# Inputs laid out on the host as they are read, a new order for the first batch's attention, and N of the second batch in 256 columns

## The chip, the cores and the metric

The kernel runs on one core of a Trainium2 chip. The metric is device time in microseconds from start to end of one execution; the median of three runs is given. The core has TensorE (matmul), VectorE, ScalarE, GpSimd and SyncE, which issues the DMAs. In the rows they are PE (PEld for its weight loads), DVE, ACT, POOL and SP.

## The reference

q, k, v are (4, 8, 576, 64) in float32; the weights w_in1, w_in2 (512, 2048) and w_out1, w_out2 (2048, 512) come as float64. Per batch and head a Nystrom attention with 32 landmarks is computed, then two feed-forward layers over 2304 tokens of width 512:

```
q_lm, k_lm = means over 18 tokens           # 32 landmarks each
A = softmax(q k_lm^T / 8);  B = softmax(q_lm k_lm^T / 8);  C = softmax(q_lm k^T / 8)
Z = B^T / (norm1(B) * norminf(B));  6 times: Z = 2 Z - Z B Z
x = A Z C v                                  # heads side by side: 2304 x 512
h = x w_in1;  x = (h * clip(h + 3, 0, 6) / 6) w_out1
h = x w_in2;  out = elu(h) w_out2
```

## The kernel before, in words

Except for the first half batch's product with w_out1, which is a plain float32 matmul, the layers' operands are split into a high and a low part (nh/nl, ath/atl, gh/gl, wo pairs) and three products are summed. The weights arrive as float64 and are converted on the chip: `steps` loads 512 doubles per partition into a staging tile (u, un or ub), ScalarE makes two passes, VectorE two (a shift and a combination, through a PSUM bank in the stream), GpSimd adds.

Attention and first layer are fused: M = Z C v (mt) is multiplied into w_in1 (tile w1c), giving N (`attn_n`, pair nh/nl), and a slot of the first layer multiplies N with A transposed (`attn_at`, pair ath/atl). There are 128 slots: batch b, half of the batch (288 tokens), 128 columns of the 2048. `slot_a1` makes h and the activation g (or gh/gl), `slot_a2` multiplies it with w_out1, DELAY = 3 slots later. Batch 0's attention is in `start`, whose order is the string PLAN, one letter a step: k prepares a pair of heads, a, b, c are the scores A, B, C of the first group of four heads, A, B, C those of the second, v and V the products with v, i a step of the inverse, f finish (which writes mt), n a block of N, t attn_at, x and y a conversion step on ScalarE and VectorE, w a fill matmul whose result nobody reads, digits and l load a weight unit. Batch 0's first half of slots (`first_half`) converts the rest of w_in1 and w_out1, two units per slot in most slots. In the second half the attention of batch 1 is woven in by the string PLAN1, where s is a fifth of a slot and n a block of N of batch 1. On VectorE, ScalarE, GpSimd and TensorE the instructions of this part run strictly in the written order (`InOrder`). After that a planner sets the order by due times (`wanted`): batches 2 and 3 (`newton`), and the conversion of the second layer's weights (`conv_out2`, `conv_in2`, every third slot).

The second layer works on 768 tokens at a time with a seven-product scheme (`quartet`, `second`). `load_x` fetches x in four pieces per half, forms four sums and splits seven operands; `load_in2` does the like for a slice of w_in2.

q and k in batch 0 are loaded as [96 partitions, 2 heads, 6 x 64] and turned by TensorE against an identity, after a copy that brings pairs of heads together (side); in batches 1 to 3 they are loaded in runs of 128 bytes (qkraw) and turned by VectorE in 32 x 32 blocks.

Of the kernel before, what the change touches and what calls it, by code (L numbers as in the profile page):

```python
# [31 lines left out]
def nystrom_ffn_kernel(ctx: ExitStack, tc, q, k, v, w_in1, w_out1, w_in2, w_out2, out):  # L32
# [28 lines left out]
    B, H, S, D = q.shape  # L61
    DM, DFF = w_in1.shape
    NT = B * S
    G = H // 4
# [5 lines left out]
    NDM = DM // 128  # L70
# [105 lines left out]
    def heads(x, b, g, pr):  # L176

        return x[b].rearrange("(i r) t d -> r i t d", r=G)[g, 2 * pr:2 * pr + 2]

# [18 lines left out]
    def steps(src, u, f, out=None):  # L198
# [3 lines left out]
        if isinstance(src, list):  # L202
            n = W // len(src)
            for i, x in enumerate(src):
                gated(sp.dma_start(
                    out=u[:, i * n:i * n + n].rearrange("p (k n) t -> p k (n t)", k=x.shape[1]), in_=x.bitcast(U32)
                ))
            lo, hi = u[:, :, 0], u[:, :, 1]
        elif len(src.shape) == 3:
            u = u.rearrange("p (k n) t -> p k n t", k=src.shape[1])  # L210
            sp.dma_start(out=u.rearrange("p k n t -> p k (n t)"), in_=src.bitcast(U32))
# [81 lines left out]
    ROOM = [{3: "nl1"}, {0: "nh2", 1: "nl2", 2: "nh3", 3: "nl3"}, {3: "nl3"}, {}]  # L293

    def conv_in1(c):

        def unit(o):
            if (0, c) not in w1_t:
                w1_t[0, c] = w1_tile()
            t = w1_t[0, c]  # L300
            cols = slice(c * W + o, c * W + o + 128)
            f = t[:, o // 128]
            yield from steps(w_in1[:, cols].rearrange("(k p) n -> p k n", p=128), room(ROOM[c].get(o // 128)), f)
# [29 lines left out]
    def conv_in2(m, kk):  # L333

        w = w_in2.rearrange("(h k p) (i n) -> h k p i n", h=2, p=128, i=2)[:, kk, :, :, m * 128:m * 128 + 128]
        src = [w[h, :, i:i + 1] for h, i in ((0, 0), (1, 0), (1, 1), (0, 1))]
        sp.dma_start(out=wi2d[m, kk], in_=to_f32(src, room()))
# [60 lines left out]
    def load_qk(b, g, what, prs=range(2)):  # L398
        src = k if what == "k" else q
        for pr in prs:  # L400
            t = ap_.tile([128, TB, 32], F32, name="qkraw", tag="qkraw", bufs=4)
            for hp in range(2):
                for e in range(2):
                    p0 = 32 * (2 * hp + e)
                    gated(sp.dma_start(
                        out=t[p0:p0 + 32],
                        in_=heads(src, b, g, pr)[hp, :, 32 * e:32 * e + 32].rearrange("(tb t) d -> t tb d", t=32),
                    ))
            raw_t[b, g, what, pr] = t

    def load_v(b, g, tiles=None):

        if tiles is None:
            vt = ap_.tile([128, 4, RUN * D], F32, name="vt", tag="vt", bufs=1)
            tiles = [vt[:, 0:2], vt[:, 2:4]]
        for i in range(2):
            sp.dma_start(
                out=tiles[i][0:PRUN],
                in_=heads(v, b, g, i).rearrange("h (p j) d -> p h (j d)", j=RUN),
            )  # L420
# [20 lines left out]
    def landmarks(x, lm, bd):  # L441

        vec.tensor_reduce(
            out=lm, in_=x.rearrange("p (l c) -> p l c", c=POOL), axis=AX, op=ALU.add
        )
        pool.tensor_tensor(
            out=bd, in0=lm.unsqueeze(1).to_broadcast([128, 2, 32]),
            in1=maskp.unsqueeze(2).to_broadcast([128, 2, 32]), op=ALU.mult,
        )

    def lm_tiles(b, g, what):
        lm = ap_.tile([128, 2, 32], F32, name="lm", tag="lm" + what, bufs=2 if what == "k" else 1)
        if what == "k":
            kl_t[b, g] = lm
        t = ap_.tile([128, 2, 2, 32], F32, name="bd", tag="bd", bufs=3)
        (kbd_t if what == "k" else qbd_t)[b, g] = t
        return lm, t

    def prep(b, g):

        for what, dst in (("k", kt_t), ("q", qt_t)):
            x = ap_.tile([128, 2, S], F32, name=what + "t", tag=what + "t")
# [3 lines left out]
            nb, ng = (b, g + 1) if g + 1 < G else (b + 1, 0)  # L466
            if nb < B:
                load_qk(nb, ng, what)
            lm, t = lm_tiles(b, g, what)
            for pr in range(2):  # L470
                landmarks(x[:, pr], lm[:, pr], t[:, pr])
                yield 1.3
            dst[b, g] = [x[:, pr, :] for pr in range(2)]
# [5 lines left out]

    def load_first(src, g, tiles):  # L480

        for i in range(2):
            sp.dma_start(
                out=tiles[i][0:PRUN],
                in_=heads(src, 0, g, i).rearrange("h (p j) d -> p h (j d)", j=RUN),
            )
        return tiles

    def prep_first():

        JB = RUN // 2
        pairs = [(g, what, pr) for g in range(G) for what in "kq" for pr in range(2)]
        sides = []

        def beside(i):

            g, what, pr = pairs[i]
            src = raw_t[0, g, what][pr].rearrange("p h (j d) -> p j h d", d=D)
            for x in ("gh", "gl"):
                t = gp.tile([128, JB * 2 * D], F32, name="side", tag=x)  # L500
                (vec.tensor_copy if x == "gh" else act.copy)(
                    out=t[0:PRUN].rearrange("p (j h d) -> p j h d", j=JB, h=2),
                    in_=src[0:PRUN, JB * (x == "gl"):JB * (x == "gl") + JB],
                )
                sides.append(t)

        beside(0)
        beside(1)
        for i, (g, what, pr) in enumerate(pairs):
            dst = kt_t if what == "k" else qt_t  # L510
            if pr == 0:
                if g == 0:
                    n = "h" if what == "k" else "l"
                    dst[0, g] = [
                        nat.tile([128, G, W], F32, name="kq", tag=f"n{n}{2 + j}").rearrange("p g w -> p (g w)")[:, 0:S]
                        for j in range(2)
                    ]
                else:
                    t = ap_.tile([128, 2, S], F32, name=what + "t", tag=what + "t")
                    dst[0, g] = [t[:, j] for j in range(2)]  # L520
                lm, bd = lm_tiles(0, g, what)
            x = dst[0, g][pr]
            xj = x.rearrange("p (t j) -> p j t", j=RUN)
            for a in range(2):
                b = bank()[:, 0:JB * PRUN]
                for j in range(JB):
                    atr(b[:, PRUN * j:PRUN * j + PRUN], sides[2 * i + a][0:PRUN, 2 * D * j:2 * D * (j + 1)],
                        ident[0:PRUN, 0:PRUN])
                act.copy(out=xj[:, JB * a:JB * a + JB], in_=b.rearrange("p (j t) -> p j t", j=JB))
            if i + 2 < len(pairs):  # L530
                beside(i + 2)
            landmarks(x, lm[:, pr], bd[:, pr])
            yield
# [16 lines left out]
    def score_c(b, g, sc):  # L550
# [16 lines left out]
        for hf in range(2):  # L567
# [3 lines left out]
            )  # L571
        return EC

    def soft(b, g):
# [3 lines left out]
        for hf in range(2):  # L578
# [4 lines left out]
            yield 0.4  # L583
        ea = ap_.tile([128, TB, 32], F32, name="ea", tag="ea", bufs=2)
# [177 lines left out]
    PLAN = "kkkkkk3bykbykcyc1bcll02ByBBwwyxlaccwwywiyyxyaaivwwywCixyvyiylaCixviCiyyCvwyiiAyaAvAiiVAyvVvyyiVyiVyViVaiwyAiyyyyyxyfAAVwywwxwfAyxfywyyyyxnwxt"  # L762

    def start():
# [10 lines left out]

        def fill(eng):
# [9 lines left out]
            "k": prep_first, "f": lambda: finish(0, kept["Q"], cvs, sc), "n": lambda: attn_n(0, 0, 128),  # L786
            "i": lambda: keep("Q", inverse(EB, sb)),
# [9 lines left out]
        for c in PLAN.replace(" ", ""):  # L797
# [5 lines left out]
            elif c == "t":  # L803
                run(attn_at(0, 0, vec))
# [4 lines left out]
            else:  # L809
                if c not in gens:  # L810
                    gens[c] = make[c]()
                next(gens[c], None)
        return units, gens["n"]
# [246 lines left out]
    def loads(b):  # L1060
        load_v(b, 0)
        for what in "kq":
            for pr in range(2):
                yield
                load_qk(b, 0, what, [pr])
# [47 lines left out]
    PLAN1 = "ssssssuulslullslsssspppspsssppspppssssosssbbcsbsocscscsaPasvaoavsssPvvosPavPasssPossPssPPssssssssBPoCCBssCBososssisCsssisAississiAoAssissisVosiVAVVioiAsssAVisisisiioisssfftftssssnotsnTnssonnssnonsnsssnnsnnsTnnosssnnsssTssssssss"  # L1113

    def second_half(slots):
# [7 lines left out]
        def parts():  # L1123
            for c in range(NW):
                yield from attn_n(1, c, 128)
# [155 lines left out]
```

## Time and profile before

| | us |
|---|---|
| median of 3 runs | 862.93 (862.11 to 863.07) |
| the profiled execution | 861.07 |
| its span, first to last instruction | 859.2 |
| TensorE, VectorE, ScalarE, GpSimd busy | 817.8, 532.1, 465.2, 346.5 |
| mean granted TensorE clock | 0.974 |

The profiled execution's own time is 1.87 us over its span, and 1.86 us under the median. A granted clock of 1.00 is 2.4 GHz, 0.50 is 1.2 GHz; values between them are mixtures over the stretch. DMA share is the busy share of the 16 DMA engines as the profile counts it, and it can read slightly over 1.

### The profile page before, as it was taken

To read this page: it belongs to the slowest core of one execution; us is meant where nothing else is said; L and a number is where in the kernel's file an instruction comes from. 1 tells how busy PE (TensorE), PEld (TensorE's weight loads), DVE (VectorE), ACT (ScalarE), POOL (GpSimd) and SP (SyncE) were. 2 spreads that over 40 slices of the span, in tenths; PEclk is the share of its full clock that TensorE was granted. 3 is DMA by queue.
4 is the path that set the end of the run, shared out by engine and by line. 5 is a ranking of instruction groups with operands and counts; after the bars stand their busy time and mean duration, and the time that the engine had idled before them with its cause. 6 is when DMAs were issued, how large, how long until landed. Compare 5 with 4: busy or idle time off the path is not lost.

```text
span 859.2 us, 16284 instructions
## 1 busy us (share of the span) xinstructions
PE 817.8 (95%) x5896; PEld 708.2 (82%) x5896; DVE 532.1 (62%) x1080; ACT 465.2 (54%) x1048; POOL 346.5 (40%) x352
## 2 busy tenths in 40 slices
PE   7788899889999999999998899999999999999998
PEld 5556687679887788979998789999889889999996
DVE  6789687536664465445776887664665555645544
ACT  7578455444554555557565666564454444434433
POOL 1357566425553365547576885631082000000000
PEclk9969999969999999999999899999999999999999
DMA  9868996358455633366387557768665365664541
GB/s 258 263 221 290 249 179 91 104 169 211 127 156 172 225 114 103 99 194 199 128 285 263 177 184 252 272 241 300 228 212 202 135 208 209 202 229 168 172 147 73
DMA packets 167024, 165.69 MB, mean 193 GB/s; under 512 B 64801, under 2 KB 129825, under 8 KB 166945
## 3 DMA queue, kind: packets, MB, share of 16 engines
q1 hardware_dynamic: 166944, 164.66, 61.0%
q8 instruction: 46, 0.75, 0.4%
q14 instruction: 34, 0.27, 0.1%
HBM read 119.54 MB, written 45.09 MB: 192 GB/s over the span
## 4 chain that ended last, share of the span: by engine, by line
PE 68%; DVE 10%; DMA 9%; ACT 4%; issue 3%; POOL 3%; SPq 2%; DVEq 0%; POOLq 0%; ACTq 0%
PE x L104 35%; PE h L104 26%; PE bk L104 8%; DMA u<-in_moe_w_out 3%; SPq L104 2%; DMA u<-in_moe_w_in 2%; DVE y L104 1%; DVE u L104 1%; DVE h L104 1%; POOL x L104 1%; DMA out<-ob 1%; DVE gf L104 1%; DVE w1c L104 1%; DVE nl L104 1%; DMA x<-x1d 1%
## 5 line engine op out<-in xcount | busy, mean ns | idle before, releaser
L104 PE MATMUL h<-x,wi 128*128 128x384 f32 x1008 | 207.8, 341 | 7.1 <-DVE y L104 3.1
L104 PE MATMUL x<-gh,wo 128*128 128x288 f32 x896 | 205.8, 303 | 0.0
L104 PEld LDWEIGHTS h<-x,wi 128*128 128x128 f32 x1008 | 182.6, 190 | 22.7 <-DVE y L104 4.4
L104 PEld LDWEIGHTS x<-gh,wo 128*128 128x128 f32 x896 | 152.3, 191 | 15.2 <-issue 13.4
L104 PE MATMUL x<-gl,wo 128*128 128x288 f32 x448 | 134.3, 301 | 0.6 <-POOL gl L104 0.3
L104 ACT CAST gh<-gf 128x288 fp32r<-128x288 f32 (+1 forms) x172 | 79.0, 460 | 81.1 <-DVE gf L104 80.7
L104 PE MATMUL x<-w,gh 128*128 128x512 f32 x360 | 116.3, 393 | 0.0
L104 ACT ACTIVATE gf<-y 128x384 f32<-128x384 f32 x96 | 50.4, 525 | 99.2 <-DVE y L104 99.2
L104 POOL TENSOR_TENSOR gl<-gf,gh 128x288 fp32r<-128x288 f32 x84 | 68.9, 823 | 77.7 <-ACT gh L104 73.3
L104 DVE SCALAR_TENSOR_TENSOR gf<-gf,y 128x384 f32<-128x384 f32 x96 | 63.6, 663 | 57.7 <-ACT gf L104 57.6
L104 PE MATMUL h<-atl,nh 128*128 128x288 f32 x256 | 83.1, 324 | 12.5 <-DVE g L104 8.8
L104 PEld LDWEIGHTS x<-gl,wo 128*128 128x128 f32 x448 | 85.4, 191 | 6.0 <-issue 4.0
L104 PE MATMUL x<-w,ghl 128*128 128x512 f32 x324 | 89.2, 392 | 0.0
L104 ACT ACTIVATE gf<-h,half_b 128x288 f32<-128x288 f32 x128 | 64.0, 500 | 40.2 <-PE h L104 37.6
L104 PE MATMUL h<-ath,nh 128*128 128x288 f32 x256 | 78.0, 305 | 0.0
L104 DVE SCALAR_TENSOR_TENSOR gf<-gf,h 128x288 f32<-128x288 f32 x112 | 49.9, 446 | 45.2 <-ACT gf L104 44.5
L104 PE MATMUL h<-ath,nl 128*128 128x288 f32 x256 | 77.6, 303 | 0.0
L104 PEld LDWEIGHTS x<-w,gh 128*128 128x128 f32 x360 | 67.5, 189 | 9.2
L104 DVE TENSOR_TENSOR gl<-gf,gh 128x384 fp32r<-128x384 f32 (+1 forms) x88 | 59.2, 673 | 25.5 <-ACT gh L104 21.4
L104 PE MATMUL x<-w,gl 128*128 128x512 f32 x180 | 70.9, 394 | 0.0
L104 PEld LDWEIGHTS h<-atl,nh 128*128 128x128 f32 x256 | 49.9, 195 | 23.6 <-DVE g L104 13.0
L104 PEld LDWEIGHTS x<-w,ghl 128*128 128x128 f32 x324 | 60.2, 188 | 8.4
(158 smaller groups left out, 1349.3 us busy)
## 6 DMA issues: line engine op xcount, KB each, us to landing
wi<-wi2p SPq DMA_DIRECT2D x64, 448.0 KB, 4.9
w<-wo2p SPq DMA_DIRECT2D x32, 512.0 KB, 6.2
wi2p<-wi SPq DMA_DIRECT2D x32, 448.0 KB, 2.8
w1c<-w1d SPq DMA_DIRECT2D x48, 256.0 KB, 4.1
ub<-in_moe_w_out SPq DMA_DIRECT2D x16, 512.0 KB, 7.2
u<-in_moe_w_out SPq DMA_DIRECT2D x16, 512.0 KB, 4.5
wo2p<-w SPq DMA_DIRECT2D x16, 512.0 KB, 3.1
u<-in_moe_w_in SPq DMA_DIRECT2D x64, 128.0 KB, 2.8
```

The costliest lines, as they stand in the source:

```text
L104: inst = getattr(self.eng, name)(*a, **kw)
```

## The change

The host now lays q and k out as [batch, group, 128, 2, 576] (head dimension on partitions, tokens in the row), v as [batch, group, 96, 4, 384], w_in1 in blocks of 128 columns with each partition's four runs together, and w_in2 in the order in which `conv_in2` reads it. So `load_qk` is one DMA, `prep_first` with its matmuls and copies and VectorE's transposes in `prep` are gone, and one DMA replaces four in `conv_in2`. PLAN is new, k prepares both pairs of heads, and one y pair stands where there were many. N of batch 1 is made in blocks of 256 columns, with eight n in PLAN1 in place of sixteen. Not in the title: two staging places differ in ROOM, the loads of q and k for batches 2 and 3 are issued in `score_c` and `soft`, `load_x(0)` subtracts on VectorE where it used GpSimd, and `load_in2(1)` is due four slots later.

```diff
-        if isinstance(src, list):
-            n = W // len(src)
-            for i, x in enumerate(src):
-                gated(sp.dma_start(
-                    out=u[:, i * n:i * n + n].rearrange("p (k n) t -> p k (n t)", k=x.shape[1]), in_=x.bitcast(U32)
-                ))
...
+            gated(sp.dma_start(
+                out=u.rearrange("p n t -> p (n t)"), in_=src.rearrange("p k n -> p (k n)").bitcast(U32)
+            ))
...
-    ROOM = [{3: "nl1"}, {0: "nh2", 1: "nl2", 2: "nh3", 3: "nl3"}, {3: "nl3"}, {}]
+    ROOM = [{2: "nl1", 3: "nh1"}, {0: "nh2", 1: "nl2", 2: "nh3", 3: "nl3"}, {3: "nl3"}, {}]
...
-    def load_qk(b, g, what, prs=range(2)):
-        src = k if what == "k" else q
-        for pr in prs:
-            t = ap_.tile([128, TB, 32], F32, name="qkraw", tag="qkraw", bufs=4)
-            for hp in range(2):
-                for e in range(2):
...
+    def load_qk(b, g, what):
+        t = ap_.tile([128, 2, S], F32, name=what + "t", tag=what + "t", bufs=2)
+        gated(sp.dma_start(out=t, in_=(k if what == "k" else q)[b, g]))
+        raw_t[b, g, what] = t
...
             for pr in range(2):
-                gated(vec.transpose(out=x[:, pr], in_=raw_t.pop((b, g, what, pr)).rearrange("p a c -> p (a c)")))
-                yield 1.3
...
+                gated(vec.tensor_reduce(
+                    out=lm[:, pr], in_=x[:, pr].rearrange("p (l c) -> p l c", c=POOL), axis=AX, op=ALU.add
+                ))
...
-    def prep_first():
...
+        if 0 < b < B - 1:
+            load_qk(b + 1, g, "k")
         return EC
...
-    PLAN = "kkkkkk3bykbykcyc1bcll02ByBBwwyxlaccwwywiyyxyaaivwwywCixyvyiylaCixviCiyyCvwyiiAyaAvAiiVAyvVvyyiVyiVyViVaiwyAiyyyyyxyfAAVwywwxwfAyxfywyyyyxnwxt"
+    PLAN = """
+        k0k1k23bbllccllkb cc BBB CCCC aaAA ixxi vavvVivv
+        iVai iVAwwi iVAawwwi iVawwwi ixxywwwi A iywwwwii
+        ffAwwwwwtxfxwwwwntwwwwwxt
+    """
...
-    PLAN1 = "ssssssuulslullslsssspppspsssppspppssssosssbbcsbsocscscsaPasvaoavsssPvvosPavPasssPossPssPPssssssssBPoCCBssCBososssisCsssisAississiAoAssissisVosiVAVVioiAsssAVisisisiioisssfftftssssnotsnTnssonnssnonsnsssnnsnnsTnnosssnnsssTssssssss"
+    PLAN1 = "ssssssuulslullslsssspppspsssppspppssssosssbbcsbsocscscsaPasvaoavsssPvvosPavPasssPossPssPPssssssssBPoCCBssCBososssisCsssisAississiAoAssissisVosiVAVVioiAsssAVisisisiioisssfftftssssotsnTssonssnosnsssnsnsTnosssnsssTssssssss"
...
-                yield from attn_n(1, c, 128)
+                yield from attn_n(1, c, 256)
...
-                x0 = load_x(0, pool)
+                x0 = load_x(0, vec)
...
-    wanted(NA - 6)
+    wanted(NA - 2)
     load_in2(1)
...
+        if name in ("q", "k"):
+            b, h, s, d = a.shape
+            a = a.reshape(b, 2, 2, h // 4, s, d).transpose(0, 3, 2, 5, 1, 4).reshape(b, h // 4, 2 * d, 2, s)
+        elif name == "v":
+            b, h, s, d = a.shape
+            a = a.reshape(b, 4, h // 4, s // 6, 6 * d).transpose(0, 2, 3, 1, 4)
+        elif name == "moe_w_in":
+            a = a.reshape(a.shape[0] // 128, 128, a.shape[1] // 128, 128).transpose(2, 1, 0, 3)
+        elif name == "moe2_w_in":
+            a = a.reshape(2, 2, 128, 2, a.shape[1] // 256, 128).transpose(4, 1, 2, 0, 3, 5)
+            a = _np.stack([a[:, :, :, i, j] for i, j in ((0, 0), (1, 0), (1, 1), (0, 1))], axis=3)
```

## Rows read from the trace of the kernel before

**Rows 1.** The page, part 1: busy us (share of span) x instructions.
```profile
PE 817.8 (95%) x5896; PEld 708.2 (82%) x5896; DVE 532.1 (62%) x1080; ACT 465.2 (54%) x1048; POOL 346.5 (40%) x352
```
**Rows 2.** Stretches: length, busy (x instructions) by engine, clock, DMA share, GB/s.
```profile
700.00:800.00 100.00, 100.00 (x500) 90.53 (x499) 54.06 (x101) 44.53 (x89) 0.00 (x0) 1.00 0.56 196
```
**Rows 3.** VectorE in order of time: start, duration, instruction.
```profile
37.64 0.28 DVE L104 COPY mt<-bk 128x128 f32<-128x128 f32 x1
...
64.97 0.45 DVE L104 SCALAR_TENSOR_TENSOR g<-gf,h 128x288 f32<-128x288 f32 x1
...
68.88 0.45 DVE L104 SCALAR_TENSOR_TENSOR g<-gf,h 128x288 f32<-128x288 f32 x1
...
101.93 0.46 DVE L104 SCALAR_TENSOR_TENSOR g<-gf,h 128x288 f32<-128x288 f32 x1 [0.43 <-ACT gf L104]
```
**Rows 4.** Waits of TensorE, 105 to 300 us: total, times, longest.
```profile
PE bk L104 <- DVE nl L104: 5.7, 8, 0.7
```
**Rows 5.** Stretches around the N of batch 1.
```profile
160.00:170.00 10.00, 7.79 (x139) 5.35 (x139) 4.81 (x18) 5.61 (x21) 4.19 (x5) 1.00 0.47 132
170.00:180.00 10.00, 8.18 (x98) 5.67 (x98) 3.74 (x14) 3.71 (x15) 2.40 (x3) 0.65 0.76 228
180.00:190.00 10.00, 9.27 (x77) 7.64 (x76) 2.48 (x9) 4.56 (x15) 2.52 (x4) 0.66 0.23 78
```
**Rows 6.** The stretch ahead of the second layer.
```profile
385.00:445.00 60.00, 57.82 (x418) 54.79 (x417) 38.70 (x64) 38.97 (x88) 41.54 (x37) 0.97 0.57 181
```
**Rows 7.** TensorE's groups, 0 to 20 us: busy, mean ns, idle before.
```profile
L104 PE MATMUL bk<-ident,side 96*128 96x96 f32 x48 | 9.5, 373 | 5.1 <-DVE side L104 4.9
```
**Rows 8.** The first 18 us in order of time, ScalarE and VectorE.
```profile
3.99 0.51 ACT L104 COPY side<-kqv 96x384 f32<-96x384 f32 x1 [1.97 <-DMA kqv<-in_k]
...
5.12 0.51 ACT L104 COPY side<-kqv 96x384 f32<-96x384 f32 x1 [0.62 <-DMA kqv<-in_k]
...
16.30 0.75 DVE L104 TENSOR_REDUCE lm<-qt 128x32 f32<-128x576 f32 x1
```
**Rows 9.** Stretches of 5 us in the head.
```profile
5.00:10.00 5.00, 4.75 (x27) 3.78 (x26) 3.87 (x7) 4.88 (x11) 0.59 (x2) 1.00 1.08 253
...
25.00:30.00 5.00, 4.05 (x110) 2.43 (x109) 4.36 (x15) 2.26 (x8) 1.87 (x2) 1.00 1.05 373
...
35.00:40.00 5.00, 2.01 (x37) 1.23 (x40) 4.93 (x11) 2.94 (x7) 2.52 (x3) 1.00 0.44 153
40.00:45.00 5.00, 3.41 (x39) 1.89 (x26) 3.72 (x11) 3.98 (x11) 1.48 (x2) 0.50 0.19 56
```
**Rows 10.** VectorE's groups, 0 to 105 us.
```profile
L104 DVE TENSOR_SCALAR h<-ub 128x512 uint32<-128x512 uint32 x13 | 9.0, 690 | 0.3
...
L104 DVE TENSOR_SCALAR w1c<-w1c 128x512 uint32<-128x512 uint32 x3 | 1.2, 402 | 0.1
```
**Rows 11.** 53 to 60 us in order of time, TensorE and VectorE.
```profile
53.54 3.83 PE L104 MATMUL x<-g,ub 128*128 128x288 f32 x8
...
58.14 0.49 DVE L104 TENSOR_TENSOR nl<-bk,nh 128x128 fp32r<-128x128 f32 x2 [2.73 <-ACT nh L104]
```
**Rows 12.** The tile nh: duration ns min/median/max, starts, forms.
```profile
L104 ACT CAST nh<-bk x80: 259/271/599, 38.6 to 388.4; 128x128 fp32r<-128x128 f32 x64, 128x512 fp32r<-128x512 f32 x16
L104 DVE TENSOR_TENSOR nl<-bk,nh x80: 275/290/694, 39.2 to 389.2; 128x128 fp32r<-128x128 f32 x64, 128x512 fp32r<-128x512 f32 x16
```
**Rows 13.** VectorE's groups, 105 to 200 us.
```profile
L104 DVE STREAM_TRANSPOSE kt<-qkraw 128x576 f32<-128x576 f32 x8 | 5.8, 759 | 0.0
```
**Rows 14.** GpSimd's groups, 385 to 445 us (two of four).
```profile
L104 POOL TENSOR_TENSOR x<-u,x 128x384 fp32r<-128x384 f32 x8 | 8.6, 1082 | 0.2 <-ACT x L104 0.2
...
L104 POOL TENSOR_TENSOR u<-x,u 128x384 f32<-128x384 f32 x6 | 6.9, 1153 | 0.3
```
**Rows 15.** VectorE in order of time, one subtraction.
```profile
438.80 0.46 DVE L104 TENSOR_TENSOR gl<-gf,gh 128x288 fp32r<-128x288 f32 x1 [0.66 <-ACT gh L104]
```
**Rows 16.** VectorE's groups, 385 to 445 us.
```profile
L104 DVE TENSOR_TENSOR gl<-gf,gh 128x288 fp32r<-128x288 f32 x19 | 14.4, 756 | 8.2 <-ACT gh L104 7.7 <-PE h L104 0.5
```

More of the change, by code (lines that the diff above doesn't have):

```diff
@@ L69, in nystrom_ffn_kernel @@
     NKT = DFF // 128
-    NDM = DM // 128
     RUN = 6
@@ L302, in unit @@
             f = t[:, o // 128]
-            yield from steps(w_in1[:, cols].rearrange("(k p) n -> p k n", p=128), room(ROOM[c].get(o // 128)), f)
+            yield from steps(w_in1[c * MPC + o // 128], room(ROOM[c].get(o // 128)), f)
             yield sp, 2
@@ L333, in conv_in2 @@
     def conv_in2(m, kk):
-        w = w_in2.rearrange("(h k p) (i n) -> h k p i n", h=2, p=128, i=2)[:, kk, :, :, m * 128:m * 128 + 128]
-        src = [w[h, :, i:i + 1] for h, i in ((0, 0), (1, 0), (1, 1), (0, 1))]
-        sp.dma_start(out=wi2d[m, kk], in_=to_f32(src, room()))
+        f = stg.tile([128, W], F32, name="y", tag="y", bufs=YB)
+        run(steps(w_in2[m, kk], room(), f.rearrange("p (k n) -> p k n", k=4)))
+        sp.dma_start(out=wi2d[m, kk], in_=f)
     def scratch(n, w):
@@ L414, in load_v @@
             vt = ap_.tile([128, 4, RUN * D], F32, name="vt", tag="vt", bufs=1)
-            tiles = [vt[:, 0:2], vt[:, 2:4]]
+            sp.dma_start(out=vt[0:PRUN], in_=v[b, g])
+            v_t[b, g] = [vt[:, 0:2], vt[:, 2:4]]
+            return
         for i in range(2):
[L417 to L420, printed above, removed]
+            sp.dma_start(out=tiles[i][0:PRUN], in_=v[b, g, :, 2 * i:2 * i + 2])
         v_t[b, g] = tiles
@@ L478, in spare @@
         return t[:, 0:2 * RUN * D].rearrange("p (h j) -> p h j", h=2)
[L480 to L487, printed above, removed]
-    def prep_first():
[L491 to L533, printed above, removed]
     def score_b(b, g, sb, EB):
@@ L774, in start, with preps @@
         units += [[conv_out1(kk), None] for kk in range(NFILL)]
+        def preps():
+            for g in range(G):
+                yield from prep(0, g)
         def fill(eng):
@@ L785, in start @@
         make = {
-            "k": prep_first, "f": lambda: finish(0, kept["Q"], cvs, sc), "n": lambda: attn_n(0, 0, 128),
-            "i": lambda: keep("Q", inverse(EB, sb)),
+            "k": preps, "f": lambda: finish(0, kept["Q"], cvs, sc), "n": lambda: attn_n(0, 0, 128),
+            "i": lambda: keep("Q", inverse(EB, sb)), "t": lambda: attn_at(0, 0, vec),
         }
@@ L796, in start @@
         gens = {}
-        for c in PLAN.replace(" ", ""):
+        for c in "".join(PLAN.split()):
             wanted(-60)
@@ L812, in start @@
                 next(gens[c], None)
+        run(gens["t"])
         return units, gens["n"]
@@ L1061, in loads @@
         load_v(b, 0)
-        for what in "kq":
-            for pr in range(2):
+        for g in range(G):
+            for what in "kq":
                 yield
-                load_qk(b, 0, what, [pr])
+                load_qk(b, g, what)
     def first_half(units, n0):
@@ L1152, in nystrom_ffn_kernel @@
     wanted(-70)
-    for i, (g, what) in enumerate((g, what) for g in range(G) for what in "kq"):
-        raw_t[0, g, what] = load_first(k if what == "k" else q, g, [spare(4 + 2 * i + pr) for pr in range(2)])
-    wanted(-55)
+    for g in range(G):
+        for what in "kq":
+            load_qk(0, g, what)
+    wanted(-65)
     for g in range(G):
```

64 lines of the change are left out of this document (23 added, 41 removed).

## The prediction

> **What bounds the kernel now.** I read the page first, then tables of stretches, then the order of time on single engines. The page says TensorE is busy for 95% of the span [rows 1], but that is an average over stages with different limits. From about 105 us on, TensorE is the bound: in a late stretch of 100 us it is busy for all of it [rows 2], and nothing done to another engine can shorten that. So a gain can only come from three places where TensorE waits or runs at half clock.
>
> The first place is the head. Until batch 0's attention has produced mt (copied at 37.64 us) no FFN slot can run; then sixteen slots follow, each ending its first half with a g on VectorE, the last of them at 101.93 us [rows 3]. Two neighbouring g stand at 64.97 and 68.88, so a slot takes 3.9 us; VectorE's pieces in it (two float64 weight units at 2 x 0.69 us each, the split of N, g) come to about 3.6 us, and VectorE runs them back to back. TensorE is not the limit there.
>
> The second place is the stretch where the N of batch 1 is made. Between 105 and 300 us TensorE waited 8 times, 5.7 us in all, for the eviction nl of such a block [rows 4], and after a stretch with TensorE busy 7.8 of 10 us the granted clock shows 0.65 and 0.66 in 170 to 190 us [rows 5]: mostly the level of 1.2 GHz instead of 2.4.
>
> The third is the passage from the first FFN to the second: between 385 and 445 us TensorE loses 2.2 us, and GpSimd is busy 41.5 of 60 us [rows 6].
>
> **The change, part by part.** *Head.* Removed for batch 0: VectorE's 8 and ScalarE's 8 side copies, ScalarE's 16 copies from PSUM, and 48 transposing matmuls in the trace (9.5 us of TensorE, with 5.1 us of waiting in front) [rows 7]. All of it lay between the landing of the data and the last landmark reduction, which ends at 16.30 + 0.75 = 17.05 us [rows 8]. What is left in front of that reduction is the landing itself and eight reductions of 0.75 us. Each new k or q tile is 128 x 1152 x 4 = 0.59 MB. In 5 to 10 us the queue moved 253 GB/s at full DMA share; in 25 to 30 us, with weight rows, 373 [rows 9]. Today the first tile of 0.29 MB is used at 3.99 us and the second at 5.12 [rows 8], so I put the first 0.59 MB at 5.1 us. At 253 GB/s each further tile takes 2.33 us: the fourth lands at 12.1, two reductions follow, 13.6, which is 3.4 us earlier. At 373 GB/s a tile takes 1.58 us and, starting at 4.5, the fourth lands at 9.2 and the last reduction ends at 10.7, 6.3 us earlier. The chain from there to mt keeps its steps (scores, maxima, six Newton rounds, finish), but its order now holds two conversion instructions of VectorE instead of the six that the trace has in it (three units of two [rows 10]); with two extra ScalarE fills against me I take 1.1 us for that. So mt comes 4.5 to 7.4 us earlier; I take 5.5, closer to the slow end, because the k and q tiles are moved in the same first 10 us.
>
> That order also defers work: two of the three units converted before mt now stand in front of the first g, 2 x 2 x 0.69 = 2.8 us of VectorE that had been covered by waiting [rows 10]. Net -2.7 us at the first g. From there the slots run at VectorE's pace as before, so the lead is kept. One hole may close: at 53.54 us a group of x matmuls ran 3.83 us at half clock, and VectorE then stood idle 2.73 us for the next block of N [rows 11]. The clock had fallen after 35 to 40 us, where TensorE was busy 2.0 of 5 us [rows 9]. The new order has 29 fill matmuls where the old one has 16, most of the new ones around finish. I count half of the hole, -1.4. **Head: -4.1 us** (bounds -7.4 + 2.8 - 2.8 = -7.4, and 0 if the weights then arrive no earlier and the slots wait for them).
>
> The Trainium skill (Perfetto Trace Analysis, DMA Optimizations) says that larger transfers, 2 KB raised to 4 KB or more, saturate HBM better; here rows go from 1.5 KB to 4.6 KB for k and q and from 1 KB to 4 KB for w_in. By that rule the fast landing holds and the head gives -7.4 + 2.8 - 1.4 = -6.0. The rows bear it out only in part: 373 GB/s was reached with many 1 KB rows in flight [rows 9].
>
> *N of batch 1 in 256 columns.* Sixteen rounds become eight, of the same number of matmul columns. A round is TensorE, then ScalarE nh, then VectorE nl, twice, with both banks held. With 128 columns these take 0.27 and 0.29 us; with 512 columns 0.60 and 0.69 at most [rows 12]. For 256 I put 0.38 and 0.43, between them by length, so the banks are held 0.38 + 0.38 + 0.43 = 1.2 us after TensorE instead of 0.27 + 0.27 + 0.29 = 0.8. The written order now has no two n next to each other: of seven gaps three hold one slot step, two hold two, two hold three. A step is about 0.5 us of TensorE, so the gaps expose 3 x 0.7 + 2 x 0.2 = 2.5 to 2.8 us against 5.7 now: -2.9. If a step covered nothing, eight waits of 1.2 us, 9.6, would be +3.9. The clock: 0.35 x 10 + 0.34 x 10 = 6.9 us of lost speed, at 87% busy 6.0 [rows 5]. Whether it stays up depends on the gaps that are left; I take 2.5. The block transposes of batch 1 (0.76 us each on VectorE [rows 13]) and their short-row loads also go, but TensorE was full beside most of them: -0.5. **This part: -5.9 us** (bounds -9.4 and +3.9).
>
> The Trainium skill (TensorE: Matmul & The Clock Gate, A second HAM failure mode: psum-queue depth-cycling) speaks against the clock term: cycling through PSUM banks with short idles between groups of matmuls makes the clock go back and forth. By that rule the clock falls here too and this part is -3.4.
>
> *load_x(0) on VectorE, load_in2(1) four slots later, one DMA for four in w_in2.* GpSimd loses 22 subtractions of about 1.1 us, in four groups of 8, 6, 6 and 2 [rows 14]: 24 us. VectorE gets them at 0.45 us (a 288-column subtraction took 0.46 where it ran undisturbed [rows 15]) to 0.61 (the same by 384 columns for 288): 10 to 13 us in a stretch where it is busy 38.7 of 60 [rows 6]. But the slots' gl there average 0.76 us over 19, against that 0.46 [rows 15, 16]; I put the difference on GpSimd's traffic, 5.7 us that would come back. What hides the rest is VectorE's 21 us of idle time, if the subtractions fall into it. I take **-1 us**, half of the 2.2 us that TensorE loses, with bounds -2.2 (all of it) and +13.4 (all 22 at 0.61 in front of a gf that TensorE needs). On SyncE's queue four DMAs of a w_in2 unit become one and eight of a k or q group become one, so no load stands behind more issues than before, and I cost the queue at nothing; what covers it is TensorE's full stretch, and if the load for the next batch's k, now issued in score_c, waits there for its buffer, the w1c loads behind it are late next. Later batches also lose their block transposes and short-row loads; TensorE has little idle time there: **-0.5**.
>
> **Sum.** -4.1 - 5.9 - 1 - 0.5 = -11.5. The profiled execution took 861.07 us, so 849.6; the median of the runs is 1.86 us above it, so I predict 851.4.
>
> **The rivals.** (1) The clock falls as before in both places: head -2.7, N -3.4, the rest -1.5, sum -7.6: 855.3. For it: the rows show half clock behind both places, and neither place loses all its waits [rows 5, 9]. Against: there are fewer of them. The Trainium skill's rule on the clock, above, would make it this case. (2) The head's lead is lost, because weights land no earlier and slots wait for them. Today the DMA share is only 0.44 and 0.19 in 35 to 45 us [rows 9], so loads were ahead, which speaks against it. Head 0: 855.5. (3) All goes well: fast landing, clock up at both places, -7.4 - 9.4 - 2.2 - 0.5: 843.4. (4) Slower: the 22 subtractions stand in VectorE's queue in front of the slots' gf and gl, and the slots of batch 3 run at VectorE's pace. At full price +13.4, while the rest keeps -10.5: +2.9, 865.8. It decides for slower by 0.2% once 12.2 of the 13.4 us are exposed. Against it: 21 us of idle time on VectorE, and three slots of lead between a gl and the matmul that reads it. (5) The wider blocks don't remove waits: +3.9 in place of -5.9 there leaves -1.7: 861.2, the same within error.
>
> **How the numbers follow.** The forecast's case (847 to 856) 0.42, rival 1 0.20, rival 2 0.10, rival 3 0.13, rival 4 0.11, rival 5 0.04. A difference under 0.2% (1.7 us) can't be told from none here. Faster: 0.42 + 0.20 + 0.10 + 0.13 = 0.85; the same 0.04; slower 0.11. The range 844 to 861 leaves out rival 4, and about half of the cases at its ends. For the forecast's own case it is 847 to 856.
>
> **What would show it.** Head: mt copied near 32 us, and the sixteenth g near 98. If mt is early but the g are not, the deferred conversions or the loads took it back. If VectorE waits for k or q past 12 us, the landing was mis-sized. N: eight rounds, TensorE's wait for nl near 2.8 us, and no stretch of 10 us at a clock of 0.65. Passage: GpSimd's busy time in the 60 us ahead of the second FFN down by 24 us and gl near 0.5; VectorE over 95% there with TensorE waiting for gf would be rival 4. The prediction is wrong as a whole if TensorE, full from 105 us on, has more to do per slot afterwards, for example at a lower clock.

## The result: slower, and the profile after

The changed kernel takes 871.06 us (median of 868.29, 870.79, 871.33 and 872.62) against 863.00 for the kernel before: ratio 1.0091, interval 1.0064 to 1.0118, so a small loss, but one clear of noise. The forecast was 851.4, so both sign and size are wrong, and the time lies above every rival too (rival 4 gave 865.8). The profiled execution took 872.62 us, with a span of 870.8.

To see where the time went I cut both traces at the same four events, each at its start: ScalarE's last copy xs of the first half batch, of the second, of the eighth, and TensorE's last matmul h<-x,wi of the second layer.

| stage (us) | before | after | difference |
|---|---|---|---|
| A: start to the end of half batch 1 (head and sixteen slots) | 113.6 | 119.0 | +5.4 |
| B: half batch 2 (attention of batch 1 and its N) | 73.8 | 64.8 | -9.0 |
| C: half batches 3 to 8 (N of batches 2 and 3) | 289.8 | 306.1 | +16.3 |
| D: to the last h of the second layer | 367.2 | 366.0 | -1.2 |
| sum | 844.4 | 855.9 | +11.5 |

The two profiled executions lie 11.6 us apart, their medians 8.1, so some 3 us of the differences are scatter between executions. Stage B gained more than forecast, A lost where a gain was forecast, and C, which was costed at -0.5, lost 16.3 us. The page's first part answers to [rows 1]:

```profile
PE 824.6 (95%) x5746; PEld 704.2 (81%) x5746; DVE 519.2 (60%) x1054; ACT 450.9 (52%) x1008; POOL 321.9 (37%) x330
```

150 matmuls fewer, and TensorE is busy 6.8 us longer. That is the first sign: something on TensorE became dearer. TensorE's groups by shape, 0 to 500 us (busy, mean ns | idle before), give its name:

```profile
L109 PE MATMUL bk<-w1c,mt 64*32 64x512 f32 x128 | 32.5, 601 | 0.0
...
L109 PE MATMUL bk<-w1c,mt 64*32 64x128 f32 x256 | 8.1, 315 | 6.1 <-POOL w1c L109 6.1
L109 PE MATMUL bk<-w1c,mt 64*32 64x256 f32 x128 | 6.2, 388 | 1.5 <-DMA w1c<-w1d 1.5
```

The first row is N of batches 2 and 3, whose code the change does not touch. The same 128 instructions at the same mean of 601 ns were busy 14.9 us in the kernel before:

```profile
L104 PE MATMUL bk<-w1c,mt 64*32 64x512 f32 x128 | 14.9, 601 | 0.6 <-DVE nl L104 0.6
```

An instruction is no dearer; they overlap less. A block is sixteen of them, each on 64 rows and 32 columns of the array, so that they can stand side by side. TensorE in order of time, in one block of the changed kernel:

```profile
261.57 1.04 PE L109 MATMUL bk<-w1c,mt 64*32 64x512 f32 x2
262.55 0.40 PE L109 MATMUL h<-ath,nl 128*128 128x288 f32 x1
262.87 1.04 PE L109 MATMUL bk<-w1c,mt 64*32 64x512 f32 x2
263.85 0.40 PE L109 MATMUL h<-ath,nh 128*128 128x288 f32 x1
264.18 1.04 PE L109 MATMUL bk<-w1c,mt 64*32 64x512 f32 x2
...
268.08 1.06 PE L109 MATMUL bk<-w1c,mt 64*32 64x512 f32 x6
```

A pair alone takes 1.04 us, six take 1.06. The planner has put a slot's full-width matmul behind nearly every pair. Counted over all eight blocks of the trace, the 128 matmuls stand in 31 unbroken runs; in the kernel before they stood in 14 (six times a pair and fourteen, twice sixteen). 32.5 / 31 and 14.9 / 14 are both about 1.05 us per run. No busy share shows it, since TensorE counts as busy all the while: the late stretch of [rows 2] is as full as before, and so is 385 to 445 us, the answer to [rows 6], where GpSimd has lost its 24 us as forecast:

```profile
385.00:445.00 60.00, 59.78 (x405) 52.47 (x405) 39.18 (x74) 36.44 (x83) 18.15 (x17) 1.00 0.41 136
```

In stage B the stretches of [rows 5] are whole, the clock stands at 1.00, and among TensorE's waits from 105 to 300 us nl, the 5.7 us of [rows 4], does not appear any more:

```profile
160.00:170.00 10.00, 9.14 (x96) 6.56 (x95) 6.46 (x16) 4.68 (x13) 6.28 (x7) 1.00 0.09 25
170.00:180.00 10.00, 8.46 (x109) 5.47 (x112) 4.63 (x12) 5.65 (x16) 3.13 (x4) 1.00 0.88 249
180.00:190.00 10.00, 10.00 (x88) 8.48 (x73) 5.21 (x14) 7.16 (x20) 6.46 (x9) 1.00 0.81 246
```

In the head, VectorE in order of time (in square brackets: idle before, and what ended it):

```profile
10.38 1.41 DVE L109 TENSOR_REDUCE lm<-qt 128x32 f32<-128x576 f32 x2 [0.58 <-DMA qt<-in_q]
...
24.48 0.22 DVE L109 TENSOR_TENSOR X<-X,bk 128x64 f32<-128x64 f32 x1 [4.91 <-ACT X L109]
...
28.25 0.22 DVE L109 TENSOR_TENSOR X<-X,bk 128x64 f32<-128x64 f32 x1 [1.64 <-ACT X L109]
...
31.21 0.22 DVE L109 TENSOR_TENSOR X<-X,bk 128x64 f32<-128x64 f32 x1 [1.57 <-ACT X L109]
...
37.48 0.25 DVE L109 COPY mt<-bk 128x128 f32<-128x128 f32 x1
...
48.86 0.45 DVE L109 SCALAR_TENSOR_TENSOR g<-gf,h 128x288 f32<-128x288 f32 x1
```

The last landmark reduction ends at 11.79 us against 17.05 [rows 8]: the lead of 5.3 us is there. At mt it is gone (37.48 against 37.64 [rows 3]), and the first g comes at 48.86. The start of the loss stands on ScalarE and TensorE:

```profile
18.38 0.50 ACT L109 ACTIVATE EC<-bk,mx 128x288 f32<-128x288 f32 x1 [4.04 <-PE bk L109]
```
```profile
20.96 0.54 PE L109 MATMUL bk<-kqv,ect 96*32 96x64 f32 x24 [2.67 <-ACT ect L109]
```

EC has one buffer. The second group's exponentials stand in ScalarE's written order and wait 4.04 us until TensorE has transposed the first group's EC, which it does only at 17.38. Behind them stand two conversions and the copies ect; TensorE waits for these, and Newton's first round, whose X is ready at 18.91, runs at 23.52. Between mt and the first g a second wait comes in, of TensorE from 36 to 60 us (total, times, longest), which the kernel before does not have:

```profile
PE bk L109 <- POOL w1c L109: 6.1, 2, 4.1
```

The blocks of N wait there for units of w_in1 that are still being converted.

### The profile page after: what moved, and what is told of

Its sections match the earlier page's. It is cut to its first block, busy times and chain, and to the rows that moved or that the text cites. A ratio compares the mean times of both kernels' runs of the same rounds, so it can differ in the third digit from the quotient of the medians.

```text
span 870.8 us, 15636 instructions
## 1 busy us (share of the span) xinstructions
PE 824.6 (95%) x5746; PEld 704.2 (81%) x5746; DVE 519.2 (60%) x1054; ACT 450.9 (52%) x1008; POOL 321.9 (37%) x330
## 4 chain that ended last, share of the span: by engine, by line
PE 74%; DVE 7%; DMA 5%; POOL 4%; ACT 2%; issue 2%; SPq 0%; DVEq 0%; POOLq 0%; ACTq 0%
PE x L109 39%; PE h L109 28%; PE bk L109 7%; DVE h L109 1%; DMA kt<-in_k 1%; POOL x L109 1%; DMA out<-ob 1%; POOL xf L109 1%; DMA x<-x1d 1%; DVE w1c L109 1%; DVE y L109 1%; DVE gf L109 1%; DMA u<-in_moe_w_in 1%; DMA w1c<-w1d 1%; SPq L109 0%
## 5 line engine op out<-in xcount | busy, mean ns | idle before, releaser
L109 PE MATMUL x<-gl,wo 128*128 128x288 f32 x448 | 131.8, 296 | 1.3 <-DVE gl L109 1.3
L109 DVE SCALAR_TENSOR_TENSOR gf<-gf,y 128x384 f32<-128x384 f32 x96 | 64.5, 672 | 59.0 <-ACT gf L109 59.0
L109 DVE TENSOR_TENSOR gl<-gf,gh 128x384 fp32r<-128x384 f32 (+1 forms) x88 | 57.6, 658 | 19.6 <-ACT gh L109 15.0
```

The costliest lines, as they stand in the source:

```text
L109: inst = getattr(self.eng, name)(*a, **kw)
```

## The experiments

The theory has two parts. (1) The due times of batches 2 and 3 moved, because each landmark sum of `prep` lost a companion yield of 1.3, and with them the planner broke up the blocks of N. (2) The head's lead is lost in the written order. Rivals: load_x(0) on VectorE (the prediction's rival 4), the host's layout itself, and due times that cost time by other ways than the grouping. Stages are cut as above; "N" is the busy time of the 128 matmuls in 512 columns in the run's profile, with the number of unbroken runs in which they stand.

| run | median us | ratio to before (95% interval) | A | B | C | D | N, runs |
|---|---|---|---|---|---|---|---|
| before | 863.0 | | 113.6 | 73.8 | 289.8 | 367.2 | 14.9, 14 |
| after | 871.06 | 1.0091 (1.0064 to 1.0118) | 119.0 | 64.8 | 306.1 | 366.0 | 32.5, 31 |
| e1 due times back | 859.12 | 0.9945 (0.9921 to 0.9968) | 118.8 | 63.9 | 289.3 | 370.7 | 14.9, 14 |
| e2 N due 4 slots earlier | 853.46 | 0.9880 (0.9835 to 0.9925) | 118.2 | 64.3 | 287.0 | 366.6 | 15.8, 14 |
| e3 load_x back | 872.50 | 1.0105 (1.0070 to 1.0141) | 117.9 | 64.0 | 306.8 | 366.3 | 32.5, 31 |
| e4 before, N in 256 | 850.94 | 0.9846 (0.9796 to 0.9897) | 113.2 | 62.8 | 291.2 | 367.5 | 15.6, 14 |
| e5 blocks kept whole | 860.67 | 0.9973 (0.9949 to 0.9997) | 116.5 | 63.9 | 294.7 | 370.9 | 10.2, 8 |
| e6 before, due times cut | 863.59 | 0.9991 (0.9963 to 1.0019) | 113.8 | 73.8 | 294.1 | 367.6 | 20.1, 19 |
| e7 = e2, no fills | 851.46 | 0.9866 (0.9823 to 0.9909) | 119.0 | 67.1 | 288.4 | 366.5 | 14.9, 14 |
| e8 = e2, head reordered | 848.10 | 0.9825 (0.9789 to 0.9860) | 116.3 | 64.1 | 285.1 | 366.5 | 14.9, 14 |
| e9 = e2, second order | 844.04 | 0.9795 (0.9762 to 0.9829) | 110.8 | 64.5 | 286.3 | 367.1 | 14.9, 14 |
| e10 = e9, load_x back | 851.01 | 0.9875 (0.9833 to 0.9916) | 110.4 | 63.8 | 290.3 | 367.7 | 14.9, 14 |
| e11 = e9, due times back | 854.74 | 0.9904 (0.9864 to 0.9943) | 109.4 | 63.8 | 290.3 | 371.8 | 14.9, 14 |
| e12 = e9, three blocks of four whole | 855.99 | 0.9928 (0.9895 to 0.9961) | 109.1 | 63.8 | 295.2 | 369.1 | 9.9, 8 |

Each ratio is against runs of the kernel before on the same chip: e1 to e4 and e9 to e11 ran on one chip, e5 to e8 on a second, e12 on a third. Those runs of the kernel before lay between 855.97 and 869.60 us, so a difference under some 3 us can't be read from medians. Stages come from one execution each and scatter too: five runs with the changed kernel's head (after, e1, e2, e3, e5) have A from 116.5 to 119.0.

**e1: the due times given back.**

```diff
                 if b or pr:
                     yield 1.3
+                if b > 1:
+                    yield 1.3
```

> The changed kernel, with the halves of due time that the shorter preparation no longer counts given back for batches 2 and 3 (a bare yield of 1.3 behind each landmark sum; no instruction is added or taken away). In TensorE's program order each block of N of these batches then stands together again (six as one pair and fourteen, two as sixteen, as in the kernel before), where the changed kernel has 22 lone pairs. Theory (the strips lose their running side by side when a full-width matmul stands between them): busy time of the 128 matmuls of 512 columns from 32.5 us back to about 15, and the whole from 871 to 853 to 857, so faster than the kernel before. Rival 1 (the loss is load_x(0) on VectorE and the passage): 869 to 872. Rival 2 (the loss is the head and the host's layout): 869 to 872.

Measured: 859.12 us, N back at 14.9 us. TensorE in order of time, two blocks:

```profile
262.52 1.09 PE L109 MATMUL bk<-w1c,mt 64*32 64x512 f32 x16
267.69 1.04 PE L109 MATMUL bk<-w1c,mt 64*32 64x512 f32 x2
269.25 1.08 PE L109 MATMUL bk<-w1c,mt 64*32 64x512 f32 x14
```

Sixteen together take 1.09 us, as long as a pair alone. No instruction was added or taken out, and stage C falls by 16.8 us, about as N does (17.6). The whole is 12 us below the changed kernel, not the 14 to 18 expected, since stage D is 4.7 us longer: TensorE waits 4.9 us for u and 2.7 us for the copy a at the passage (2.0 and 1.8 in the changed kernel).

**e2: N of batches 2 and 3 due four slots earlier.**

```diff
+            wanted(i - 4)
             run(attn_n(b + 1, (r - NKT) // MPC - 1))
+            wanted(i)
```

and the same around the block issued at r == 0.

> The changed kernel, with the due time of N of batches 2 and 3 put four slots earlier and nothing else. It brings the same grouping in TensorE's order (six times a pair and fourteen, twice sixteen) by another edit, with the preparation's due times left as the change has them. Theory (grouping of N alone): busy time of the N matmuls of 512 columns about 15 us, whole time 853 to 858, within 3 us of the run with the due times given back. Rival (the due times of the preparation and of Newton themselves cost the time, not the grouping): near 866 to 871, while the run with the due times given back gains.

Measured: 853.46 us, N 15.8 us, stage C 287.0. Another edit with the same grouping gives the same saving, with prep's due times left as the change has them; so what stage C lost is the grouping. All nine kernels with 14 runs have C between 285.1 and 291.2 us, the two with 31 (after and e3) 306.1 and 306.8. It is better than e1 by 2.3 us in stage C and 4.1 in D; the medians lie 5.7 us apart, not within the expected 3.

**e3: load_x(0) on GpSimd again, and load_in2(1) due at NA - 6.**

> The changed kernel, with load_x(0) on GpSimd again and the second quarter of the second FFN's weights due six slots ahead of the end again, as in the kernel before. N stays scattered in TensorE's order. Theory (N's scatter and the head are the loss): 869 to 873, the 128 matmuls of N still near 32 us. Rival (the 22 subtractions in front of the slots on VectorE are the loss, the fourth rival of the prediction): 857 to 861.

Measured: 872.50 us, stage D 366.3 against 366.0. The 22 subtractions are not the loss.

**e4: the kernel before, with N of batch 1 in 256 columns and the new PLAN1.**

```diff
-                yield from attn_n(1, c, 128)
+                yield from attn_n(1, c, 256)
```

> The kernel before, with N of batch 1 alone in 256 columns and the order of the second half that goes with it; host layout, head, preparation and passage are those of before. Theory (this part of the change is worth what the half batch showed, 8.9 us): 853 to 856, the waits for nl between 100 and 200 us gone, clock 1.00 in 160 to 200 us. Rival (the wider blocks gain only together with the shorter head or the missing transposes): 860 to 864.

Measured: 850.94 us, 12 to 13 us under the kernel before and below the 853 to 856 expected; stage B alone 11.0 us shorter. TensorE's group, 110 to 190 us:

```profile
L104 PE MATMUL bk<-w1c,mt 64*32 64x256 f32 x128 | 6.4, 388 | 0.6 <-DVE nl L104 0.4 <-DMA w1c<-w1d 0.2
```

With 128 columns the same group took 10.0 us there with 5.1 us of waiting for nl:

```profile
L104 PE MATMUL bk<-w1c,mt 64*32 64x128 f32 x256 | 10.0, 323 | 5.2 <-DVE nl L104 5.1
...
162.98 0.64 PE L104 MATMUL bk<-w1c,mt 64*32 64x128 f32 x16 [0.73 <-DVE nl L104]
...
164.54 0.45 PE L104 MATMUL bk<-w1c,mt 64*32 64x128 f32 x16
...
176.91 0.87 PE L104 MATMUL bk<-w1c,mt 64*32 64x128 f32 x16 [0.73 <-DVE nl L104]
```

So 3.6 us come from the matmuls themselves and 4.7 from the waits. Part of the 3.6 is the clock: a block behind such a wait took 0.64 us at a granted clock of 1.00 and 0.87 at 0.50 (175 to 180 us), which, with the blocks between, makes about 1.3 us over the last six. Some 2.3 are left for half as many runs of sixteen, and for fewer that start behind a wait (0.64 us, against 0.45 without one). The 2.7 that are left of the 11.0 I put down to the clock too, which stays at 1.00 from 160 to 190 us here; no run shows them apart.

**e5: every block kept whole, due times as changed.** Slot matmuls issued before the block must stand ahead of it, later ones behind it.

```diff
+    def smm(*a):
+        inst = mm(*a)
+        if fence[0] is not None:
+            after(inst, fence[0])
+        recent.append(inst.ins)
+        return inst
...
-                marks["slot"] = mm(ps, w[:, g, o:o + 128], x[:, g, :], n == 0, n == 3 * G - 1).ins
+                marks["slot"] = smm(ps, w[:, g, o:o + 128], x[:, g, :], n == 0, n == 3 * G - 1).ins
```

In `attn_n` the block's first matmul depends on the last 18 of recent, and its last becomes fence[0].

> The changed kernel, with due times as the change has them, and every slot matmul kept out of N's blocks of batches 2 and 3: those issued earlier stand ahead of the block in TensorE's order, the later ones behind it. All eight blocks are then one run of sixteen. Theory (a run of strips side by side costs about 1.05 us whatever its length: 31 runs cost 32.5 us in the changed kernel, 14 runs 14.9 us in the kernel before): 8 runs cost 8 to 9 us, and the whole falls by about 24 us to 845 to 849. Rival (a block that can't be broken up holds the slots back until its banks and w1c are there, so that TensorE waits for what the grouping saves): 852 to 858.

Measured: 860.67 us, above the rival's range too. N falls to 10.2 us in eight runs: six took 1.09 us each, the two that open a batch, each behind a wait for mt, 1.75 and 1.96. But of 22.3 us saved on N, 11.4 reach the end of stage C, and stage D is 4.9 us longer, so the rival has the direction right. TensorE's waits from 200 to 400 us show two of the places:

```profile
PE x L109 <- ACT xs L109: 3.7, 3, 1.9
PE bk L109 <- DVE Qd L109: 3.4, 2, 1.8
```

As I read them, a block that can't be passed makes the slots behind it wait for what N itself waits for.

**e6: the kernel before, with the same due times cut.**

```diff
                 landmarks(x[:, pr], lm[:, pr], t[:, pr])
-                yield 1.3
+                if b < 2:
+                    yield 1.3
```

> The kernel before, and only the due time of the landmark sums of batches 2 and 3 no longer counted (two fewer yields of 1.3 in each tensor's preparation, no instruction changed), which is what the change did to the plan without the rest of it. In TensorE's order the 128 matmuls of N in 512 columns then stand in 19 runs instead of 14. Theory (the due times set off the scatter, 1.05 us for each run): busy time of these matmuls about 20 us instead of 14.9, and the whole 3 to 6 us longer than before. Rival (only together with the host's layout do the due times cost anything): within 1.5 us of before.

Measured: N takes 20.1 us in 19 runs, as the theory counted.

```profile
L104 PE MATMUL bk<-w1c,mt 64*32 64x512 f32 x128 | 20.1, 601 | 0.1
```

Stage C is 4.3 us longer in the profiles, but the medians, 863.59 against 864.26, show nothing. The trigger works in the old kernel too; on the whole time the medians fit the rival, and the cost is inconclusive.

**e7: e2 without the fills between the Newton rounds.** Fifteen w are taken out of PLAN (the expectation miscounts them as 13).

> As the run with N due four slots earlier (853.5), and 13 of the head's fill matmuls, those between the Newton rounds of batch 0, taken out; they compute nothing that is used. Theory (the fills stand in front of the rounds in TensorE's order and use up the lead that the earlier loads gave): mt copied at 32 to 34 us instead of 37.5, last g 3 to 4 us earlier than 107, whole 849 to 851. Rival (the rounds wait for ScalarE's work in order, and without fills TensorE's clock stays at the lower level for longer): mt at 36 to 38, whole 853 to 856.

Measured: 851.46 us; mt at 36.0, last g at 107.3, stage A 119.0. mt is 1.7 us earlier (37.7 in e2) and the sixteen slots gain nothing, so the theory fails in the head; 36.0 is where the rival put mt. The whole, 2.0 us under e2, decides nothing, and the profiled execution took 857.77 us, 6.3 above the median, so its stages, B above all, count for less. The granted clock was 0.58 and 0.57 in 20 to 30 and 30 to 40 us (0.67 and 0.82 in e2, with the fills).

**e8: e2 with another written order.** The first transposes of EC stand ahead of the second group's exponentials, Newton's first round ahead of the values, both first units are converted between the rounds, and the fills between the rounds are gone.

```diff
-        k0k1k23bbllccllkb cc BBB CCCC aaAA ixxi vavvVivv
-        iVai iVAwwi iVAawwwi iVawwwi ixxywwwi A iywwwwii
-        ffAwwwwwtxfxwwwwntwwwwwxt
+        k0k1k23bbllccllkb cc BBB CCC v C aa i AA i v i a v i v i
+        a V x i v i A V y i x i V a y i x i V A i x i a V y i y A ii
+        ff A wwwwt f ww n t wwww x x t
```

> As the run with N due four slots earlier (853.5), with the head's written order changed: the first group's transposes of EC ahead of the second group's exponentials, the first Newton rounds ahead of the values' matmuls, no fills between rounds, and both first units of w_in1 converted between the rounds instead of behind them. Theory (the lead of 5 us at the landmarks and 8 us at Newton's start is lost in the order, nothing else): mt copied at 29 to 32 us instead of 37.5, first g near 40 instead of 49, last g near 99, whole 845 to 848. Rival (the sixteen slots of the first half batch are held by the conversions, which run at the pace of the loads and of ScalarE, so that an earlier mt buys waits): mt early, but last g after 104 and the whole 851 to 854.

Measured: 848.10 us; mt at 35.1, first g 47.0, last 104.8. Stage A, 116.3, is hardly outside the 116.5 to 119.0 of the unchanged heads, and the last g is as late as the rival had it, so this order shows no clear gain in the head. VectorE's order of time shows what held mt:

```profile
29.63 0.63 DVE L109 SCALAR_TENSOR_TENSOR w1c<-u,w1c 128x512 uint32<-128x512 uint32 x1
30.18 1.37 DVE L109 TENSOR_SCALAR w1c<-w1c 128x512 uint32<-128x512 uint32 x1
31.47 0.21 DVE L109 TENSOR_TENSOR X<-X,bk 128x64 f32<-128x64 f32 x1
```

The last Newton product was done at 29.0, but its update stood behind two conversions that I had put in its way.

**e9: these moved behind Newton's last update, and the fills ahead of the first block of N taken out.**

```diff
-        a V x i v i A V y i x i V a y i x i V A i x i a V y i y A ii
-        ff A wwwwt f ww n t wwww x x t
+        a V x i v i A V x i y i V a i y i V x A i x i a V i A ii
+        f y f f A t n y t ww xx t
```

> As the run with the head's new order (848.1), with two things moved that its trace showed late: the conversions that stood on VectorE ahead of Newton's last update go behind it (the last product was done at 28.9 us, the update ran at 31.47), and the fill matmuls ahead of the first N block are gone. Theory (the head is set by each engine's written order): mt copied at 31 to 32 us instead of 35.1, first g at 40 to 43 instead of 47.0, last g near 100 instead of 104.8, whole 842 to 845. Rival (the loads behind the store of w_in1's first units pace the sixteen slots): last g after 103 and the whole 847 to 849.

Measured: 844.04 us (843.11 to 845.41), the fastest of all, 0.9795 of the kernel before and some 27 us under the changed kernel. VectorE:

```profile
29.55 0.16 DVE L109 TENSOR_TENSOR X<-X,bk 128x64 f32<-128x64 f32 x1
32.21 0.29 DVE L109 COPY mt<-bk 128x128 f32<-128x128 f32 x1 [0.46 <-PE bk L109]
41.39 0.45 DVE L109 SCALAR_TENSOR_TENSOR g<-gf,h 128x288 f32<-128x288 f32 x1
```

mt at 32.21, first g 41.4, last 99.2, stage A 8.2 us shorter than after the change: the head's lead was lost in the order. The four runs with this order (e9 to e12) have A from 109.1 to 110.8, clear of the 116.5 to 119.0 with the change's own. The slots' own pace does not move: first to last g take 57.9 us here, 58.5 after, 57.6 before.

**e10 and e11: e9 with load_x(0) back on GpSimd (and NA - 6), and e9 with e1's yields.**

> The run beside it (the head's second order, N due four slots earlier) with load_x(0) on GpSimd and the second quarter's weights due six slots ahead of the end, as in the kernel before: the passage alone, now that N is in its runs. Theory (load_x on VectorE is worth little either way): within 2.5 us of the run beside it. Rival 4 of the prediction (22 subtractions ahead of the slots' own on VectorE cost the passage): 5 to 13 us faster than the run beside it. The opposite (GpSimd is what the passage waits for): 3 us or more slower.

> The run with the head's second order, with the due times of batches 2 and 3 given back as well as N due four slots earlier; both keep N in its 14 runs. Theory (grouping is what the due times decide, the rest of the plan is worth little): within 3 us of the run beside it. Rival (the due times of before cost the second FFN's start 4 to 5 us, as in the run with them alone, 859.1 against 853.5): 4 to 6 us slower.

Measured: 851.01 and 854.74 us, 7.0 and 10.7 us above e9. So load_x(0) on VectorE together with the later load_in2(1) gains once N stands together, the opposite of rival 4; which of the two gains was not separated. In e10's profile, which took only some 4 us more than e9's, stage C carries 4.0 of it and D 0.6; TensorE's waits from 430 to 520 us:

```profile
PE h L109 <- DVE u L109: 3.5, 2, 2.2
PE h L109 <- DVE gf L109: 2.4, 2, 2.1
PE x L109 <- DVE gl L109: 1.5, 2, 1.0
```

e9 has no wait for u there, but these come after the end of stage C (464.5 us), so they do not account for its 4.0. In e11 the theory fails: with the same 14 runs, the due times of before cost 4.0 us in stage C and 4.7 in D (2.3 and 4.1 in e1 against e2). Part of what due times do is not the grouping.

**e12: e9 with three of the four blocks of each batch kept whole, as in e5.**

> The run with the head's second order and N due four slots earlier (844.0), with the later three of the four N blocks of batches 2 and 3 kept whole as in the run that kept all eight whole, where TensorE had holes around the start of a batch's N. All eight blocks are then runs of sixteen or more. Theory (1.05 to 1.3 us for a run): the N matmuls fall from 14.9 to 9 to 10 us, and 3 to 5 us of it reach the end, 839 to 841. Rival (what the whole blocks save comes back as waits of TensorE between the slots, as it did with all eight whole): 844 to 852.

Measured: 855.99 us. N falls to 9.9 us (six blocks at 1.09 us, two behind a wait for nl at 1.68), and stage C rises by 8.9 all the same: TensorE waits 6.4 us for gf and 4.7 for the copies xs from 200 to 530 us (3.2 and none in e9). The rival has the reason, and the time lies above its range: here a lone pair ahead of most blocks (1.05 us) is cheaper than a block that nothing may pass.

## Why the prediction was wrong

**The step that failed.** "Later batches also lose their block transposes and short-row loads; TensorE has little idle time there: -0.5". It asked what the change takes from TensorE in batches 2 and 3 and not what it does to TensorE's order. What the runs showed in its place: the change moved due times, the planner broke the blocks of N from 14 runs into 31, stage C cost +16.3 us and N's busy time +17.6; e1 and e2 took it back by two edits that add no work and change no operand. The diff showed the trigger: two of four yields per tensor in `prep` are gone, and `newton` adds up their values into due times. The text's own test ("TensorE, full from 105 us on, has more to do per slot afterwards") was met, but by lost overlap, not by a lower clock. The Trainium skill (TensorEngine Tiling (Array Packing), Tiling Modes, Key Properties) says that the array's small tiles run in parallel and that going from one tiling mode to another drains TensorE. The rows agree with the first, 1.04 us for a pair and 1.09 for sixteen in a row; no row here tells how much of the pair's price is the drain. At the 1.05 us per run that the rows give, 17 more runs are 18 us.

**Head, -4.1, was +5.4** (+2.7 to +5.8 over the runs with either head). The landing was right: 5.3 us earlier, inside the 3.4 to 6.3. The Trainium skill (Perfetto Trace Analysis, DMA Optimizations) says that larger transfers saturate HBM's bandwidth better. The trace agrees in the rate, 360 GB/s in 5 to 10 us against 253 [rows 9]; the lead of 5.3 us lies between the slow landing and the fast one. Wrong was "the chain from there to mt keeps its steps", with 1.1 us for the new order: EC's single buffer, ScalarE's order behind it and the deferred conversions took the whole lead and 4.5 us more at the first g. Rival 2 named the place and the wrong cause: e9 got 8.2 us back with no load moved in its issue order, and lies 2.8 under the kernel before. Fills alone are not it (e7). How the shares divide between EC, conversions, fills and the clock was not separated: the granted clock was 0.67 and 0.50 in 20 to 25 and 25 to 30 us, 1.00 in the kernel before.

**N in 256 columns, -5.9, was -9.0, and -11.0 alone (e4).** The mechanism was right, three sizes were too small: the blocks' own matmuls, counted at nothing because the columns are the same, give some 2.3 us at the same clock, since two runs of sixteen short ones cost more than one of twice the length; the waits fall by 4.7 instead of 2.9; and no clock is lost, where I had 2.5 of 6 coming back: some 4 by e4, in part a remainder. The Trainium skill (TensorE: Matmul & The Clock Gate, A second HAM failure mode: psum-queue depth-cycling) tells of a kernel whose clock went back and forth under such cycling; the granted 1.00 from 160 to 190 us, after and in e4, shows none of it in this stage. Why the changed kernel has 2.0 us less of this gain than e4 was not followed.

**The passage, -1, was -1.2 in stage D**, with GpSimd's 24 us gone as forecast. That agreement may hide a larger effect: with N together this part of the change is worth some 4 us in the profiles and 7 in the medians (e10 against e9), so the sign of rival 4 was wrong. gl on VectorE from 385 to 445 us went to 705 ns, not to 500, so most of what I had put on GpSimd's traffic did not come back.

**The rivals.** None came out. 1, 3 and 5 stay on the faster side or at no change, and only 4 gave a slower time, by a mechanism that e3 and e10 exclude.

**What stays open.** Why the planner breaks the blocks under one set of due times and not under another was not followed into the planner. e11 and e1 show a cost of due times at the passage whose cause I only place: waits for u and y on VectorE, with a clock of 0.83 in 440 to 480 us of e11. That e6's 4.3 us do not show in its medians is unexplained beyond their spread.

## What to carry to other kernels

Where a planner orders one engine's queue, an edit that only removes other engines' steps can reorder the bound engine: compare that engine's program order before and after, and the busy time of each group of the same instructions at the same mean duration. Small matmuls that share the array were priced here by the run of 2 to 16, not by the instruction; keep them together by due times, but leave the planner room to pass them (e5, e12). In a strictly written order, a lead at the start of a chain is worth nothing until each instruction ahead of the chain's next step, on every engine, has been moved or shown to be early.

## What the runs showed of the hardware

A pair of strip matmuls (64 rows, 32 columns, 512 wide) between full-width ones held TensorE for 1.04 us, sixteen in a row for 1.09, at a granted clock of 1.00, and 1.68 for sixteen behind a wait (239.86 us in e12, clock 1.00); over 14, 19 and 31 runs the busy time was 14.9, 20.1 and 32.5 us (before, e6, after). TensorE's busy share, 95% before and after, does not show such a loss. On VectorE, a TENSOR_SCALAR on w1c (128x512) took 1.37 us at 30.18 us in e8, beside a GpSimd operation on ea (128x576) that ran from 29.86 to 31.27; the same instruction took 0.42 us at 24.89 us of that run, with no GpSimd operation beside it. That GpSimd is the cause was not tested.
